# Block 0's plain columns of x: one load, or two loads on two queues, with its first products in halves

## The chip, the cores and the metric

The kernel runs on one core of a Trainium2 chip. The metric is the device time of one execution in microseconds (us). Runs of the two kernels are compared by their medians; one further execution of each is taken by the hardware profiler, and its times are those of the views quoted below. The core's engines are TensorE (PE in the views, with its weight loads as PEld), VectorE (DVE), ScalarE (ACT), GpSimd (POOL) and SyncE (SP). SP and ACT issue the kernel's loads and stores, each on a queue of its own, q1 and q10 in the views.

## The reference, cut to what matters

The output is a gated sum of two branches over x of 2048 positions and 512 features, in bfloat16:

```python
def _A_ref(x, wqkv, wo):          # sliding attention, 8 keys, 2 apart
    qkv = (x @ wqkv).reshape(B, S, 3, H, Dh)
    ...
    return o @ wo
def _B_ref(x, w1, b1, w2, b2):    # layer norm, then an MLP over the positions
    ...
g = _sigmoid((x * gate_w).sum(-1, keepdims=True))
return g * _A_ref(x, wqkv, wo) + (1 - g) * _B_ref(x, w1, b1, w2, b2)
```

The change lies in the first step of all, the product x @ wqkv for the first 512 positions.

## The kernel before, in words

The whole of x, the weights and what comes between are held on the core. Work is written as a list of operations with their engine, an estimated duration, and the names of what each reads and writes. A planner (`_Sched`) sorts them: it goes through the list by estimated start times and gives each engine one fixed order of operations, and each operation the semaphore waits that its inputs ask for. Loads have an estimated landing time in this plan (`lands`), which decides the order alone; on the chip an operation waits for the real landing. Some orders are written out by hand with `chain`.

The products contract over the 512 features in four groups of 128, called d = 0 to 3 here. As `x @ wqkv` needs x with features on the partitions, x is loaded transposed into `XT`, in blocks of 512 positions. For block 0 this is split: the features 128 to 511 (d = 1 to 3) come by a transposing load (`ld_xt0`, L473), while the features 0 to 127 (d = 0) come as they are, the plain columns, into `XP` (`d_xp`, L479). PE transposes these itself: four products with an identity (`f_tr`, L545), the first two into PSUM bank 5 (`tr0`), the other two into bank 6 (`tr1`). ACT copies the first half, positions 0 to 255, to `XT` (`ev_tra`, L555), DVE the second half, positions 256 to 511 (`ev_trb`, L557).

Ahead of the transposes, PE runs products with constants whose results nobody reads (`f_warm`, L537): six of 512 positions (`warm1`), one of 256 (`warm2`), and after the transposes one of 512 (`warm3`).

Then come the products of block 0 (`f_proj`, L619). Four banks take Q first: d = 0 for the four output tiles, then d = 1, d = 2, d = 3; then four banks take K, d = 0 and 1, then d = 2 and 3. All are of 512 positions. The first four need both copies and Wq's first quarter (rows 0 to 127 of Q's weights, `ld_w(0, 0, 1, "act")`); the second four need the transposed columns and Wq's second quarter.

The queues at the start: SP issues `d_xp`, then the transposed columns, then Wq's third and fourth quarters, K's weights in two halves, and the first tiles of x in plain form for the layer norm. ACT issues Wq's first and second quarters and then loads the table for its first activation.

Behind block 0, PE works through the other products of Q, K and V; two bursts of logit sums (L698) for which DVE multiplies Q and K (L690); the two products of the MLP (L812, L862); and the output product (L878), which DVE combines with the MLP's result (L899). The place of the bursts among PE's other products is set by the planner's estimates.

Of the kernel before, what the change touches and what calls it, by code (L numbers as in the profile page):

```python
# [333 lines left out]
def bass_gated_mix__sliding_local_dilated__mixer_token_mlp__prompt_kernel(nc, A_x, A_wqkv, A_wo, B_x, B_w1, B_b1, B_w2, B_b2, gate_w, out, dbg=None):  # L334
    with contextlib.ExitStack() as es:
# [3 lines left out]
        sch = _Sched()  # L339

        x2d = A_x[0]
        xv = x2d.rearrange("(t p) d -> p t d", p=128)
# [72 lines left out]
        A = sch.add  # L415
# [12 lines left out]
        def mk_dma(dst, src):  # L428
            return lambda e: e.dma_start(dst, src)

        init_dmas = []
# [32 lines left out]
        XT0 = ["xt0_%d" % d for d in range(4)] + ["xt0_0b"]  # L464
        ALLXT = XT0 + ["xt_%d" % t for t in range(4, NST)]

        def xt_of(sb, d0=0, d1=4):
            return XT0[d0:d1] + (XT0[4:] if d0 == 0 else []) if sb == 0 else ["xt_%d" % t for t in range(4 * sb, 4 * sb + 4)]

        def ld_xt0():  # L470
            ds = sch.dsem("xt0")
# [4 lines left out]
            return op  # L476

        XP = view("OUTS", BF16, [(128, 4), (1, 128)])
        d_xp = sch.dma("sp", mk_dma(XP, xv[:, 0:4, 0:128]), 512 * 128 * 2, sch.dsem("xp"), writes=["outs0"], issue=0.4, name="d_xp")  # L479
        d_xp.lands = 3.9  # L480
        init_dmas.append(d_xp)

        first_loads = [ld_w(0, 0, 1, "act"), ld_xt0(), ld_w(0, 1, 1, "act"), ld_w(0, 2, 1), ld_w(0, 3, 1), ld_w(1, 0, 2), ld_w(1, 2, 2),
                       ld_x(0, 2)]
        ld_xt(1)
        first_loads.append(init_dmas[-1])
        for op_, t_ in zip(first_loads, (3.5, 5.7, 5.0, 6.3, 6.7, 7.6, 8.6, 9.4, 11.0)):
            op_.lands = t_
            op_.deps.clear()
        first_loads[2].order.add(first_loads[0])  # L490
        init_dmas[:] = [first_loads[1]] + first_loads[5:]
        ld_x(2, 2)
# [8 lines left out]
        def ld_w1(j):  # L501
# [4 lines left out]
            if j < 4:  # L506
# [8 lines left out]
                       writes=["wo"], deps=throttle(), after=prev_dma(), name="d_wo")  # L515
# [4 lines left out]
        for i_, (v_, n_) in enumerate(((B_b1, NFT), (B_b2, NST))):  # L520
            vr = v_.rearrange("(t q j) -> q t j", q=4, j=32)
            for q_ in range(4):
                sch.dma("sp", mk_dma(psub(BR, 32 * q_, n_, 32 * i_, [(1, 32)]), vr[q_]), n_ * 64, ds_b, reads=["br"],
                        writes=["br_%d_%d" % (i_, q_)], deps=throttle(), after=prev_dma(), name="d_b_%d_%d" % (i_, q_), issue=0.45)
        d_w1.append(ld_w1(3))
        A("dve", lambda e: e.transpose(out=BT, in_=BR), 0.2, reads=["br_%d_%d" % (i_, q_) for i_ in range(2) for q_ in range(4)],
          writes=["btc"], name="t_b")
# [5 lines left out]
        def f_warm(n, w_=D):  # L533
            def fn(e):
                ins = None
                for _ in range(n):
                    ins = e.matmul(ps[:, 7, 0:w_], lhsT=CONE[:, 0:128], rhs=CONE[:, 0:w_], start=True, stop=True)  # L537
                return ins
            return fn

        def f_tr(h):
            def fn(e):
                ins = None
                for t in range(2):
                    ins = e.matmul(ps[:, 5 + h, 128 * t:128 * t + 128], lhsT=XP[:, 2 * h + t, :], rhs=IDENT, start=True, stop=True)  # L545
                return ins
            return fn

        A("pe", f_warm(6), 2.56, writes=["lg7_0", "lg7_1"], name="warm1", prio=-100)
        w2_ = A("pe", f_warm(1, 256), 0.2, writes=["lg7_0", "lg7_1"], name="warm2", prio=-100)  # L550
        ta_ = A("pe", f_tr(0), 0.215, reads=["outs0", "ident"], writes=["lg5_0", "lg5_1"], after=[w2_], name="tr0", prio=-100)
        tr_ = A("pe", f_tr(1), 0.215, reads=["outs0", "ident"], writes=["lg6_0", "lg6_1"], after=[ta_], name="tr1", prio=-100)
        A("pe", f_warm(1), 0.43, writes=["lg7_0", "lg7_1"], after=[tr_], name="warm3", prio=-100)
        w3_ = tr_
        A("act", lambda e: e.activation(out=XT[:, 0, 0:256], in_=ps[:, 5, 0:256], func=AF.Copy), 0.35, reads=["lg5_0", "lg5_1"],  # L555
          writes=["xt0_0"], name="ev_tra", prio=0)
        A("dve", lambda e: e.tensor_copy(out=XT[:, 0, 256:512], in_=ps[:, 6, 0:256]), 0.35, reads=["lg6_0", "lg6_1"],  # L557
          writes=["xt0_0b"], name="ev_trb", prio=0)
# [12 lines left out]
        for hf in range(2):  # L571
            t0 = 8 * hf
            for t in range(t0, t0 + 8):
                A("dve", (lambda t_: (lambda e: e.bn_stats(out=ST6[:, t_, :], in_=X[:, t_, :])))(t), 0.59,  # L574
                  reads=["x%d" % t], writes=["st6_%d" % t], name="ln1_%d" % t, prio=0)
# [13 lines left out]
              reads=["zc%d" % hf], writes=["sd%d" % hf], name="ln_sqrt%d" % hf, prio=0)  # L589
            A("dve", (lambda t0_: (lambda e: e.reciprocal(out=cols(RSTD, t0_, 8), in_=cols(SD, t0_, 8))))(t0), 0.25,  # L590
              reads=["sd%d" % hf], writes=["rstd%d" % hf], name="ln_rstd%d" % hf, prio=0)
# [40 lines left out]
        tnames = ["q", "k", "v"]  # L632
        first = [(tn, dl) for tn in range(2) for dl in range(4)]
        fbn = [["acc%d" % b] for b in range(4)] + [["lg%d_0" % b, "lg%d_1" % b] for b in range(4, 8)]
        for (b0, d0, d1, s0, s1) in ((0, 0, 1, 0, 512), (0, 1, 2, 0, 512), (0, 2, 3, 0, 512), (0, 3, 4, 0, 512), (4, 0, 2, 0, 512), (4, 2, 4, 0, 512)):
            for b in range(b0, b0 + 4):
                tn, dl = first[b]
                last_main[0] = A("pe", f_proj(tn, dl, 0, b, d0, d1, s0, s1), 0.216 * (d1 - d0) * (s1 - s0) / 512,
                                 reads=xt_of(0, d0, d1) + ["wqkv%d_%d" % (tn, dt) for dt in range(d0, d1)],
                                 writes=fbn[b], after=[last_main[0]], name="pf_%s%d_%d_%d" % (tnames[tn], dl, d0, s0))  # L640
                last_main[0].order.add(w3_)
        for b, (tn, dl) in enumerate(first):
            A("act", f_evq(tn, dl, 0, b), 0.52, reads=fbn[b] + (["k5pad"] if tn == 1 else []),
              writes=["%s5_%d_0" % (tnames[tn], dl)], name="ev_%s%d_0" % (tnames[tn], dl), prio=0)
# [7 lines left out]
        for (tn, dl, sb) in seq_proj:  # L652
# [3 lines left out]
                             reads=xr + ["wqkv%d_%d" % (tn, dt) for dt in range(4)],  # L656
# [15 lines left out]
        for t in range(NST):  # L672
# [5 lines left out]
          writes=["th"], name="g_tanh", prio=0)  # L678
# [150 lines left out]
        for ft in range(NFT):  # L829
# [6 lines left out]
              name="gel_%d" % ft, prio=0)  # L836
# [216 lines left out]
```

## Time and profile before

| | us |
|---|---|
| median of 3 runs (lowest to highest) | 167.93 (167.91 to 168.16) |
| profiled execution: its time | 168.55 |
| profiled execution: its span | 167.3 |
| PE busy in the span | 163.9 (98%) |
| DVE busy in the span | 151.3 (90%) |
| ACT busy in the span | 75.0 (45%) |

A span runs from the first to the last instruction that the profiler recorded. Matmuls are pipelined: a row's duration covers filling and draining, so the spacing of their starts, not their durations, says how fast PE works. An entry such as "idle 0.41 <-PE" names what ended the wait of an engine. In a timeline the rows are start, duration, engine, line, operation, output<-input, form and count; neighbours of one kind are merged into one row. The view of the chain that ended last is read backwards from the end of the span, and printed in order of time.

### The profile page before, as it was taken

What the parts mean: (1) busy time and instruction counts of PE and PEld (TensorE: products, weight loads), DVE (VectorE), ACT (ScalarE), POOL (GpSimd) and SP (SyncE); (2) the same over time, 40 slices, a digit from 0 to 9 for tenths busy, and PEclk for the clock granted to TensorE, in tenths of its full rate; (3) what the DMA queues carried; (4) which work ended last, traced back from release to release, by engine and by line L of the source; (5) the groups of instructions that cost most, each with busy time, mean ns of one, the idle gap of its engine ahead of it and who ended that gap; (6) DMA issues with size and microseconds to landing.
All of it is one profiled execution on the core that took longest, in us unless ns stands there. A gap on an engine that the chain in (4) does not pass through costs nothing.

```text
span 167.3 us, 2152 instructions
## 1 busy us (share of the span) xinstructions
PE 163.9 (98%) x860; PEld 77.6 (46%) x860; DVE 151.3 (90%) x154; ACT 75.0 (45%) x116; POOL 0.7 (0%) x8
## 2 busy tenths in 40 slices
PE   7999999999999999999999999999999999999994
PEld 2455555554454444444444444444444444444463
DVE  0145999999999999999999999999999999999896
ACT  3077688889899818793113121131231321310100
POOL 1000000000000000000000000000000000000000
DMA  5999999968003837996579936462672580000454
GB/s 130 315 272 262 303 322 291 307 196 246 0 0 97 311 115 187 303 290 153 133 183 343 335 129 143 112 187 68 184 218 83 138 223 0 0 0 0 157 190 159
DMA packets 47625, 29.64 MB, mean 177 GB/s; under 512 B 9856, under 2 KB 46464, under 8 KB 47616
## 3 DMA queue, kind: packets, MB, share of 16 engines
q1 hardware_dynamic: 45504, 24.85, 54.0%
q10 hardware_dynamic: 2112, 4.66, 10.0%
q8 instruction: 7, 0.11, 0.3%
q14 instruction: 2, 0.02, 0.0%
HBM read 21.24 MB, written 2.10 MB: 140 GB/s over the span
## 4 chain that ended last, share of the span: by engine, by line
PE 94%; DVE 3%; DMA 2%; issue 0%
PE ps L812 29%; PE ps L862 29%; PE ps L619 25%; PE ps L878 6%; PE ps L698 4%; DVE arena L899 2%; DMA arena<-in_A_x_dram 2%; PE ps L545 0%; DVE arena L557 0%
## 5 line engine op out<-in xcount | busy, mean ns | idle before, releaser
L812 PE MATMUL ps<-arena 128*128 128x512 bf16 x224 | 48.7, 379 | 0.0
L862 PE MATMUL ps<-arena 128*128 128x512 bf16 x224 | 48.7, 379 | 0.0
L619 PE MATMUL ps<-arena 128*128 128x512 bf16 x192 | 42.3, 382 | 0.1
L690 DVE TENSOR_TENSOR arena<-arena 128x4096 bf16<-128x4096 bf16 (+1 forms) x12 | 35.5, 2996 | 2.3 <-ACT arena L630 1.8
L797 DVE TENSOR_TENSOR arena<-arena 128x8192 bf16<-128x8192 bf16 x8 | 35.0, 4419 | 0.0
L812 PEld LDWEIGHTS ps<-arena 128*128 128x128 bf16 x224 | 21.8, 98 | 26.7 <-ACT arena L728 0.4
L862 PEld LDWEIGHTS ps<-arena 128*128 128x128 bf16 x224 | 21.9, 98 | 26.5
L619 PEld LDWEIGHTS ps<-arena 128*128 128x128 bf16 x192 | 21.6, 114 | 20.8 <-DVE arena L557 0.7
L930 ACT ACTIVATE arena<-ps,arena 128x512 bf16<-128x512 f32 x16 | 12.4, 778 | 39.4 <-PE ps L862 39.4
L800 DVE TENSOR_TENSOR arena<-arena 128x4096 bf16<-128x4096 bf16 (+1 forms) x16 | 27.0, 1752 | 0.0
L630 ACT ACTIVATE arena<-ps 128x512 bf16<-128x512 f32 x32 | 18.5, 596 | 4.5 <-PE ps L619 4.5
L833 ACT ACTIVATE arena<-ps,arena 128x512 bf16<-128x512 f32 x14 | 9.6, 687 | 22.2 <-PE ps L812 17.4
L574 DVE BATCH_NORM_STATS2 arena<-arena 128x6 f32<-128x512 bf16 x16 | 10.0, 680 | 5.6 <-DMA arena<-in_A_x_dram 5.6
L878 PE MATMUL ps<-arena 128*128 128x512 bf16 (+1 forms) x80 | 14.2, 337 | 0.0
L899 DVE SCALAR_TENSOR_TENSOR arena<-ps,arena 128x512 bf16<-128x512 f32 (+1 forms) x20 | 11.5, 638 | 0.9 <-PE ps L878 0.7
L598 ACT ACTIVATE arena<-arena 128x512 bf16<-128x512 bf16 x16 | 12.2, 806 | 0.0
L627 ACT ACTIVATE arena<-ps 128x512 bf16<-128x512 f32 x16 | 9.0, 596 | 5.5 <-PE ps L619 5.4
L878 PEld LDWEIGHTS ps<-arena 128*128 128x128 bf16 x80 | 7.8, 98 | 6.3
L674 DVE SCALAR_TENSOR_TENSOR arena<-arena 128x512 bf16<-128x512 bf16 x16 | 10.1, 685 | 0.0
L744 DVE TENSOR_TENSOR arena<-arena 128x512 bf16<-128x512 bf16 (+4 forms) x11 | 7.3, 667 | 0.6 <-ACT arena L763 0.2
L698 PE MATMUL ps<-arena 128*32 128x512 bf16 x128 | 7.3, 380 | 0.0
L728 ACT ACTIVATE arena<-ps 128x512 bf16<-128x512 f32 x8 | 4.7, 592 | 4.6 <-PE ps L698 4.6
(42 smaller groups left out, 40.5 us busy)
## 6 DMA issues: line engine op xcount, KB each, us to landing
arena<-in_B_w_dram SPq DMA_DIRECT2D x7, 1024.0 KB, 8.3
arena<-in_B_w_dram SPq DMA_DIRECT2D x8, 896.0 KB, 5.1
arena<-arena ACTq DMA_DIRECT2D x32, 128.0 KB, 3.0
arena<-in_A_x_dram SPq DMA_DIRECT2D x4, 512.0 KB, 5.1
out_dram<-arena SPq DMA_DIRECT2D x14, 128.0 KB, 1.7
arena<-in_A_x_dram SPq DMA_DIRECT2D x1, 1536.0 KB, 7.9
arena<-in_A_wqkv_dram SPq DMA_DIRECT2D x2, 256.0 KB, 3.6
arena<-in_A_x_dram SPq DMA_DIRECT2D x2, 256.0 KB, 3.5
```

What stands on the lines that cost most here:

```text
L598: A("act", (lambda t_: (lambda e: e.activation(out=X[:, t_, :], in_=X[:, t_, :], func=AF.Identity, scale=col(RSTD, t_), bias=col(NMR, t_)) ...
L619: ins = e.matmul(ps[:, bank, s0:s1], lhsT=lhsT, rhs=XT[:, dt, sb * 512 + s0:sb * 512 + s1], start=(dt == 0 and s0 == 0), stop=(dt == 3))
L630: return lambda e: e.activation(out=dst, in_=ps[:, bank, :], func=AF.Copy)
L690: return lambda e: e.tensor_tensor(out=PBL[buf][:, :, 512 * c0:512 * (c0 + nc_)], in0=in0, in1=in1, op=ALU.mult)
L698: ins = e.matmul(ps[32 * c:32 * c + 32, 4 + wl, :], lhsT=RP, rhs=PBL[buf][:, wl, c * 512:(c + 1) * 512], start=(dl == 0), stop=(dl == 3), ...
L797: A("dve", (lambda o_, i0, i1: (lambda e: e.tensor_tensor(out=o_, in0=i0, in1=i1, op=ALU.mult)))(pv, in0, in1), 4.4, reads=v_res + ["atx_% ...
L800: A("dve", (lambda pv_, n__: (lambda e: e.tensor_tensor(out=pv_[:, 0:n__], in0=pv_[:, 0:n__], in1=pv_[:, n__:2 * n__], op=ALU.add)))(pv, n ...
L812: ins = e.matmul(ps[:, bank, :], lhsT=W1W[:, slot, st, 128 * e_:128 * e_ + 128], rhs=X[:, st, :], start=(st == 0), stop=(st == NST - 1))
L862: ins = e.matmul(ps[:, bank, :], lhsT=W2S[slot][:, ft, 128 * e_:128 * e_ + 128], rhs=UT[:, ft, :], start=(ft == 0), stop=(ft == NFT - 1))
L878: ins = e.matmul(ps[:, bank, 0:c1 - c0], lhsT=OT[:, t, 128 * i:128 * i + 128], rhs=WO[:, t, c0:c1], start=(t == 0), stop=(t == 3))
L899: A("dve", (lambda i_, b_, c0_, c1_: (lambda e: e.scalar_tensor_tensor(out=T1[:, i_, c0_:c1_], in0=ps[:, b_, 0:c1_ - c0_], scalar=col(G, i ...
L930: A("act", (lambda i_, bank_: (lambda e: e.activation(out=T1[:, i_, :], in_=ps[:, bank_, :], func=AF.Identity, scale=col(OMG, i_), bias=co ...
```

## The change

`d_xp` becomes a list of two loads of 256 pieces each: the tiles 0 and 1 (positions 0 to 255) on SP, the tiles 2 and 3 on ACT, both first on their queues. `tr0` waits for the first alone, `tr1` for the second alone. Wq's first quarter is issued on ACT behind the second of them, and Wq's second quarter behind that. `warm2` is gone and `warm3` has 256 positions in place of 512; the first product of block 0 comes behind `warm3`, where it came behind `tr1` in the order that the planner was given. The four products with d = 0 for Q are cut in two: four over positions 0 to 255, which read `ev_tra`'s half alone, then four over 256 to 511, which read `ev_trb`'s. The planned landing times are given anew.

```diff
-        def xt_of(sb, d0=0, d1=4):
-            return XT0[d0:d1] + (XT0[4:] if d0 == 0 else []) if sb == 0 else ["xt_%d" % t for t in range(4 * sb, 4 * sb + 4)]
+        def xt_of(sb, d0=0, d1=4, s0=0, s1=512):
+            if sb:
+                return ["xt_%d" % t for t in range(4 * sb, 4 * sb + 4)]
+            return (XT0[d0:d1] if d0 or s0 == 0 else []) + (XT0[4:] if d0 == 0 and s1 == 512 else [])
...
-        d_xp = sch.dma("sp", mk_dma(XP, xv[:, 0:4, 0:128]), 512 * 128 * 2, sch.dsem("xp"), writes=["outs0"], issue=0.4, name="d_xp")
-        d_xp.lands = 3.9
-        init_dmas.append(d_xp)
+        d_xp = [sch.dma(q, mk_dma(XP[:, 2 * h:2 * h + 2, :], xv[:, 2 * h:2 * h + 2, 0:128]), 256 * 128 * 2, sch.dsem("xp%d" % h),
+                        writes=["outs0%s" % "ab"[h]], issue=0.4, name="d_xp%d" % h) for h, q in enumerate(("sp", "act"))]
+        for op_ in d_xp:
+            op_.lands = 3.5
+        init_dmas.append(d_xp[0])
...
-        for op_, t_ in zip(first_loads, (3.5, 5.7, 5.0, 6.3, 6.7, 7.6, 8.6, 9.4, 11.0)):
+        for op_, t_ in zip(first_loads, (4.2, 5.7, 4.7, 6.1, 6.5, 7.5, 8.4, 9.1, 11.0)):
             op_.lands = t_
             op_.deps.clear()
+        first_loads[0].order.add(d_xp[1])
         first_loads[2].order.add(first_loads[0])
...
-        A("pe", f_warm(6), 2.56, writes=["lg7_0", "lg7_1"], name="warm1", prio=-100)
-        w2_ = A("pe", f_warm(1, 256), 0.2, writes=["lg7_0", "lg7_1"], name="warm2", prio=-100)
-        ta_ = A("pe", f_tr(0), 0.215, reads=["outs0", "ident"], writes=["lg5_0", "lg5_1"], after=[w2_], name="tr0", prio=-100)
-        tr_ = A("pe", f_tr(1), 0.215, reads=["outs0", "ident"], writes=["lg6_0", "lg6_1"], after=[ta_], name="tr1", prio=-100)
-        A("pe", f_warm(1), 0.43, writes=["lg7_0", "lg7_1"], after=[tr_], name="warm3", prio=-100)
-        w3_ = tr_
+        w1_ = A("pe", f_warm(6), 2.56, writes=["lg7_0", "lg7_1"], name="warm1", prio=-100)
+        ta_ = A("pe", f_tr(0), 0.215, reads=["outs0a", "outs0", "ident"], writes=["lg5_0", "lg5_1"], after=[w1_], name="tr0", prio=-100)
+        tr_ = A("pe", f_tr(1), 0.215, reads=["outs0b", "outs0", "ident"], writes=["lg6_0", "lg6_1"], after=[ta_], name="tr1", prio=-100)
+        w3_ = A("pe", f_warm(1, 256), 0.2, writes=["lg7_0", "lg7_1"], after=[tr_], name="warm3", prio=-100)
...
-        for (b0, d0, d1, s0, s1) in ((0, 0, 1, 0, 512), (0, 1, 2, 0, 512), (0, 2, 3, 0, 512), (0, 3, 4, 0, 512), (4, 0, 2, 0, 512), (4, 2, 4, 0, 512)):
+        for (b0, d0, d1, s0, s1) in ((0, 0, 1, 0, 256), (0, 0, 1, 256, 512), (0, 1, 2, 0, 512), (0, 2, 3, 0, 512), (0, 3, 4, 0, 512), (4, 0, 2, 0, 512), (4, 2, 4, 0, 512)):
...
-                                 reads=xt_of(0, d0, d1) + ["wqkv%d_%d" % (tn, dt) for dt in range(d0, d1)],
+                                 reads=xt_of(0, d0, d1, s0, s1) + ["wqkv%d_%d" % (tn, dt) for dt in range(d0, d1)],
```

## The prediction

> **What bounds the kernel now.** I read the table of runs first, then the chain of work that ended last, then the opening of the timeline engine by engine, then the DMA queues in short windows. The profiled execution took 168.55 us, its span 167.3 us, so 1.25 us lie around the span; the median of the runs is 167.93 us. I work out a shift of the span and take it off the median. The chain in order of time (start, us, what):
>
> ```profile
> 0.80 3.10 DMA arena<-in_A_x_dram
> 3.91 0.14 issue
> 4.04 0.60 PE ps L545 x4
> 4.66 0.44 DVE arena L557
> 5.15 33.44 PE ps L619 x152
> ```
>
> The reader is to see one load (the plain columns of x, issued at 0.80, landed at 3.91), four transposes, one copy, and from 5.15 on TensorE (PE) alone. PE has no idle time worth a tenth of a microsecond behind 5.15, so what starts its products earlier moves the end, if nothing new stops it on the way. Its first products, each row the one that was running in a window of a few hundredths of a microsecond:
>
> ```profile
> 5.15 0.61 PE L619 MATMUL ps<-arena 128*128 128x512 bf16 x1
> 5.56 0.63 PE L619 MATMUL ps<-arena 128*128 128x512 bf16 x1
> 5.98 0.45 PE L619 MATMUL ps<-arena 128*128 128x512 bf16 x1
> 6.26 0.38 PE L619 MATMUL ps<-arena 128*128 128x512 bf16 x1
> 6.48 0.38 PE L619 MATMUL ps<-arena 128*128 128x512 bf16 x1
> ```
>
> The starts are 0.41, 0.42, 0.28 and 0.22 us apart: the array begins at about half rate (0.427 us for 512 positions, also the spacing of the warm-up products from 0.84) and ends at 0.216. The granted clock says 1.00 throughout, so only the spacing tells it. The 0.28 is a mixture: x at the slow rate and the rest at the fast one, x + (1 - x/0.427) 0.216 = 0.28, gives x = 0.13, so the rate rose at 5.98 + 0.13 = 6.11. A microsecond gained before 6.11 is, if the rise stays where it is, worth only 1 - 0.216/0.427 = 0.49 us at the end.
>
> **The change part by part.**
>
> *The load in two halves.* Today the one load has 512 pieces of 256 bytes. The queues in two windows, 1.9 to 2.93 and 1.9 to 3.4 (q1 is SP's, q10 ACT's; packets, bytes, share of the 16 engines):
>
> ```profile
> q10 hardware_dynamic: 95, 0.10, 34.2%
> q1 hardware_dynamic: 260, 0.07, 27.6%
> ...
> q10 hardware_dynamic: 200, 0.19, 41.4%
> q1 hardware_dynamic: 523, 0.13, 38.1%
> ```
>
> SP's queue had moved 260 packets by 2.93 and its 512 and most of the closing ones by 3.4; the load landed 0.51 after that. Half the pieces alone would land at 2.93 + 0.51 = 3.44. In the first window the engines are at 62%, so they do not pace it. Bounds for SP's half: at best it is there when PE ends the six warm-up products (3.35, the start of the seventh), at worst at 3.91 as now. ACT's half: its queue moved nothing before 2.24 (a window from 1.9 to 2.24 lists q1 alone), 0.3 later than SP's; 256 pieces at SP's 250 per us end at 3.27 and land at 3.78, at the 560 per us of 2.93 to 3.4 at 3.21. I take 3.5; the half only has to be there by 3.91 for its copy (below). The Trainium skill, "DMA: Bandwidth & Descriptors", "Issuing engines are not separate DMA queues", says that issuing on several engines saves only the time of initiating, as the same 16 engines do the work; by it the sum would be that of my first rival, 167.80. This case's trace has the engines at 62% here, so the rule's ground, engines that are full, is not met in this window.
>
> *From landing to the first product.* Now the ACT row of the evacuation:
>
> ```profile
> 0.80 1.02 ACTq L429 DMA_DIRECT2D arena<-in_A_wqkv_dram  x2
> 1.84 1.28 ACT L555 ACT_TABLE_LOAD   x1 [1.84 <-issue]
> 4.45 0.38 ACT L555 ACTIVATE arena<-ps 128x256 bf16<-128x256 f32 x1 [1.32 <-PE ps L545]
> 4.66 0.42 DVE L557 CAST arena<-ps 128x256 bf16<-128x256 f32 x1 [3.17 <-PE ps L545]
> ```
>
> ACT starts 0.54 after the landing and takes 0.38; the wait for DVE's copy ends 0.06 before the first product. The pieces need ACT's half only: 3.44 + 0.54 + 0.38 + 0.06 = 4.42, against 5.15. Bounds: 3.35 for PE free gives 4.28, and 4.5 if the wait on ACT is 0.08 slower than that on DVE (0.14 stands between landing and first transpose). ACT has one more DMA to issue, 0.43 to 0.55 by its two now, so the table load ends at 3.12 + 0.43..0.55 = 3.55 to 3.67, hidden before 3.98, when ACT is wanted. Without that cover (a landing before 3.1) it would be the next bound.
>
> *Wq's first quarter moves behind.* It is issued when the second quarter is now (1.26), which landed 3.0 later: 4.26. Bounds: 2.9 gives 4.16, a slip by one issue of 0.46 gives 4.72. With 0.14 to the product: 4.40, so the two inputs come together; I take 4.43. The second quarter moves by one issue, to about 4.8, wanted at 6.1: free.
>
> *The first four products in eight pieces.* Four more products and weight loads, the same positions: 8 x 0.213 at half rate, weight loads of 0.15 beneath (at full rate 0.108 against 0.11: at most 0.02 us in all). The last four wait for DVE's copy, which ends 1.18 behind its landing (5.09 - 3.91): 3.5 + 1.18 = 4.68, wanted at 4.43 + 0.85 = 5.28; even a landing at 3.91 hides. The shorter warm-up (one of 256 positions gone from before the transposes, one of 512 cut to 256 behind them) lies in waits: 0.21 + 0.21 us of PE off the path; its worth for the clock is a rival.
>
> *The transposed columns.* SP issues them second as now (1.29, landed 4.4 later at 5.7); behind a shorter first issue, not later. But 256 packets now stand ahead of Wq on ACT's queue, so as much of Wq falls into its time: 1519 q1 packets took 117% of 1.5 us x 16 engines in the window from 3.5 to 5.0, 0.0185 us each, so 256 x 0.0185 / 16 = 0.30 at most: 5.7 to 6.0. They are wanted after the eight pieces: 7.9 pieces at 0.213 from 4.43 reach 6.11, the rest runs at the fast rate: 6.12. Hidden, by 0.1 in the worst case. The later SP loads slip by at most 0.3 too: the second half of K's weights, issued before 5.07 and 3.6 to landing by the table of DMA issues, is there by 8.7 and wanted after twenty more products, near 10.8.
>
> *Sum.* (5.15 - 4.43) x 0.49 = 0.35 us. Does it reach the end? The rows that could stop it:
>
> ```profile
> 32.88 4.49 DVE L690 TENSOR_TENSOR arena<-arena 128x4096 bf16<-128x4096 bf16 x2
> 38.52 3.64 PE L698 MATMUL ps<-arena 128*32 128x512 bf16 x64
> 42.20 4.43 DVE L690 TENSOR_TENSOR arena<-arena 128x8192 bf16<-128x8192 bf16 x1 [0.41 <-PE ps L698]
> ...
> 157.36 0.75 DVE L899 SCALAR_TENSOR_TENSOR arena<-ps,arena 128x512 bf16<-128x512 f32 x1 [0.72 <-PE ps L878]
> ```
>
> PE's burst of logits sums at 38.52 needs DVE's products, over at 37.37: 1.15 of slack. DVE idles 0.41 for the burst's end at 42.20, so it moves along by 0.35; at the tail it waits 0.72 for PE, so it does not hold it. The plan's order behind the block: in both kernels the planner lets the second group start on the transposed columns, booked at 5.7, so its order of PE should stay. 167.93 - 0.35 = **167.58 us**.
>
> **The rivals.** *Halves that land no earlier*, or Wq late: with 3.91 the first product starts at 3.91 + 0.98 = 4.89, with Wq at 4.72 at 4.86: 0.27 x 0.49 = 0.13, so 167.80. For it: shared engines, ACT's late start; against: the 62%. *The transposed columns late*, at 6.4 instead of 5.7: the second group starts at 6.45 as now, 167.95; it needs more than twice the 0.30 worked out. *The clock rises later* (the other side): place, PE before 6.11; point, a pause before the first piece longer than the 0.30 us between the last warm-up (4.42 + 0.43 = 4.85) and 5.15, which starts the count anew. Half rate lasted 5.27 us (0.84 to 6.11); counted from 4.43 it ends at 9.70: 3.59 x 0.49 = 1.76 lost, 0.35 gained, 169.34. For it: less warm-up; against: the new pause is about 4.15 to 4.43. The Trainium skill, "TensorE: Matmul & The Clock Gate", Part 1, has a free-running window of 3.4 us that must be busy; the rise here, 5.27 us behind the first product, agrees with it, and by it one more window would end near 9.5 (an estimate). *The clock rises earlier*, if it counts work done: 0.29 us earlier, 167.43. *A burst moves by one group of products* in the plan: 0.86 later, DVE's slack of 0.72 gives way, about 167.8 or a little above 168.
>
> **How the numbers follow.** Forecast 0.62, own range 167.45 to 167.70; halves or Wq late 0.14; columns late 0.07; clock later 0.08; clock earlier 0.05; burst 0.04. What a measurement can tell here is about 0.2%, 0.34 us; the forecast lies on its edge. Faster by over 0.2% (under 167.59): 0.45 of the forecast and the early clock, 0.50. Within: 0.17 of the forecast, 0.14, 0.04 of the columns, 0.02: 0.37. Slower: 0.08 + 0.03 + 0.02 = 0.13. The range 167.3 to 168.05 takes in all but the late clock and the extremes.
>
> **What would show it.** Right: the chain's DMA piece ends at 3.4 to 3.5, ACT's L555 starts near 4.0, the first L619 row of 128x256 at 4.4 to 4.5, spacing 0.21 for eight, the first 512-wide one at 6.1 to 6.2. Wrong: a DMA piece ending at 3.9; a wait of PE on Wq or on the transposed columns after the pieces; a spacing of 0.43 beyond 6.5; a new idle row of DVE or PE behind 38.

## The result, and the profile after

| | before | after |
|---|---|---|
| median of 6 runs (lowest to highest), us | 168.16 (167.91 to 168.29) | 169.66 (168.99 to 171.21) |
| ratio of the runs, 95% interval | | 1.0100 (1.0070 to 1.0131) |
| profiled execution: time, span, us | 168.55, 167.3 | 171.21, 169.9 |

The change makes the kernel slower by 1.0%, and its runs spread over 2.2 us in place of 0.4. The ratios, here and below, leave out runs more than 1.5% above the fastest of their kernel, which the medians still count; a ratio need not equal the quotient of the two medians. The opening of the chain that ended last, after (start, us, what):

```profile
0.80 0.45 SPq L429
1.25 0.06 issue
1.31 6.26 DMA arena<-in_A_x_dram
7.57 0.05 issue
7.61 8.17 PE ps L622 x30
```

The plain columns are gone from it. In their place stands the other load of x, the transposed columns: issued at 1.31, landed at 7.57, where it had landed at 5.7. PE's own rows, and ACT's, in the timeline:

```profile
2.34 1.28 ACT L558 ACT_TABLE_LOAD   x1 [2.34 <-issue]
3.35 0.63 PE L550 MATMUL ps<-arena 128*128 128x128 bf16 x4
3.81 0.39 ACT L558 ACTIVATE arena<-ps 128x256 bf16<-128x256 f32 x1 [0.18 <-PE ps L550]
4.34 1.06 PE L622 MATMUL ps<-arena 128*128 128x256 bf16 x8 [0.23 <-DMA arena<-in_A_wqkv_dram]
7.61 0.61 PE L622 MATMUL ps<-arena 128*128 128x512 bf16 x1 [2.21 <-DMA arena<-in_A_x_dram]
```

All that the change was made for is there: the transposes start when the warm-up ends, ACT's copy at 3.81, the eight pieces at 4.34. Then PE idles 2.21 us for the transposed columns, and its second group starts at 7.61 in place of 6.48. The windows of PE's clock (us, busy time and count of PE, PEld, DVE, ACT and POOL, then PEclk, the DMA share and GB/s):

```profile
0.49:3.90 3.41, 3.06 (x11) 1.29 (x11) 0.29 (x1) 1.38 (x2) 0.56 (x5) 1.00 0.57 106
3.90:7.31 3.41, 1.27 (x10) 0.80 (x8) 0.42 (x1) 0.29 (x1) 0.00 (x0) 1.00 1.19 169
7.31:10.73 3.42, 3.12 (x8) 1.17 (x9) 0.07 (x1) 0.00 (x0) 0.00 (x0) 0.50 1.14 332
```

Here the record shows the clock: half from 7.31 to 10.73, behind the window in which PE was busy for 1.27 us of 3.41. So the second group also starts slow. (The 1.00 of the first window can't be taken at its word: the warm-up products in it start 0.42 us apart, twice the 0.216 of the full rate. The rate rose at its end, and the eight pieces start 0.11 apart.) The account of this execution: 7.61 - 6.48 = 1.13 us from the late start, and (10.73 - 7.61) x 0.49 = 1.53 from the half rate, 2.66 together; the spans differ by 2.6. The three shortest runs (168.99, 169.06, 169.39) are 0.8 to 1.2 above the median of before, about what the late start alone costs; the two longest (170.94, 171.21) are 2.8 to 3.1 above it, a little more than what both cost; 169.93 lies between. That both of the longest had the half rate fits their recorded mean clock, 0.99 in these two and 1.00 in the other four, but only 171.21 has a profile.

Why are the columns late? The queues from 3.5 to 5.0 us (packets, MB, share of 16 engines), before and then after:

```profile
q1 hardware_dynamic: 1519, 0.39, 117.2%
q10 hardware_dynamic: 51, 0.04, 7.5%
```

```profile
q1 hardware_dynamic: 646, 0.17, 64.8%
q10 hardware_dynamic: 116, 0.11, 37.8%
```

With 65 more packets on ACT's queue (q10), SP's (q1) moved 873 fewer. At the durations of before that does not balance: 65 x 0.075 x 24 / 51 = 2.3 us of the 16 engines' 24, against 873 x 1.172 x 24 / 1519 = 16 us. So the packets did not just trade places.

The experiments start from theory A: Wq's second quarter, issued 0.6 us later than before, moves on ACT's queue beside the transposing load, and slows that load and itself far beyond its own size. Its rivals: B, the two halves of x on two queues slow the load; D, the two queues only share the engines' time, as the prediction had it; P, the loss comes from the products in pieces.

### The profile page after: what moved, and what is told of

It reads as the page before. It is cut to its first block, busy times and chain, and to the rows that moved or that the text cites. A ratio compares the mean times of both kernels' runs of the same rounds, so it can differ in the third digit from the quotient of the medians.

```text
span 169.9 us, 2145 instructions
## 1 busy us (share of the span) xinstructions
PE 163.6 (96%) x849; PEld 78.2 (46%) x863; DVE 151.3 (89%) x154; ACT 75.1 (44%) x116; POOL 0.7 (0%) x8
## 4 chain that ended last, share of the span: by engine, by line
PE 92%; DMA 4%; DVE 2%; issue 1%; SPq 0%
PE ps L865 28%; PE ps L815 28%; PE ps L622 25%; PE ps L881 6%; PE ps L701 4%; DMA arena<-in_A_x_dram 4%; DVE arena L902 2%; SPq L429 0%
## 5 line engine op out<-in xcount | busy, mean ns | idle before, releaser
L865 PE MATMUL ps<-arena 128*128 128x512 bf16 x220 | 48.5, 379 | 0.2
L815 PE MATMUL ps<-arena 128*128 128x512 bf16 x219 | 48.2, 379 | 0.4 <-issue 0.2
L622 PE MATMUL ps<-arena 128*128 128x512 bf16 (+1 forms) x192 | 43.1, 384 | 2.8 <-DMA arena<-in_A_x_dram 2.2
L881 PE MATMUL ps<-arena 128*128 128x512 bf16 (+1 forms) x79 | 14.1, 336 | 0.1
L601 ACT ACTIVATE arena<-arena 128x512 bf16<-128x512 bf16 x16 | 12.2, 804 | 0.0
```

The costliest lines, as they stand in the source:

```text
L601: A("act", (lambda t_: (lambda e: e.activation(out=X[:, t_, :], in_=X[:, t_, :], func=AF.Identity, scale=col(RSTD, t_), bias=col(NMR, t_)) ...
L622: ins = e.matmul(ps[:, bank, s0:s1], lhsT=lhsT, rhs=XT[:, dt, sb * 512 + s0:sb * 512 + s1], start=(dt == 0 and s0 == 0), stop=(dt == 3))
L815: ins = e.matmul(ps[:, bank, :], lhsT=W1W[:, slot, st, 128 * e_:128 * e_ + 128], rhs=X[:, st, :], start=(st == 0), stop=(st == NST - 1))
L865: ins = e.matmul(ps[:, bank, :], lhsT=W2S[slot][:, ft, 128 * e_:128 * e_ + 128], rhs=UT[:, ft, :], start=(ft == 0), stop=(ft == NFT - 1))
L881: ins = e.matmul(ps[:, bank, 0:c1 - c0], lhsT=OT[:, t, 128 * i:128 * i + 128], rhs=WO[:, t, c0:c1], start=(t == 0), stop=(t == 3))
```

## The experiments

Eighteen kernels ran, in five jobs; in each job the kernel before ran on the same chip (medians 168.30, 168.23, 168.36, 168.50 and 168.19). "Columns" is when the transposed columns landed, "2nd group" when PE began it, in the profiled execution; it is left blank where nothing below rests on it. Each profile is of a single execution; the loads of the changed kernel, unchanged in e2 and e7, put the columns at 7.57, 7.3 and 7.8, those of the kernel before, unchanged in e1, at 5.7 and 5.8. "..." in a diff stands for lines left out. The diffs of e2, e3, e4, e6, e7 and e8 are against the kernel after, those of e1, e5 and e9 against the kernel before; the others name what they start from.

| run | columns | 2nd group | median, us | ratio to before (95%) |
|---|---|---|---|---|
| e1_pieces_only | 5.8 | 6.5 | 168.39 | 1.0001 (0.9988 to 1.0014) |
| e2_loads_only | 7.3 | 7.4 | 169.20 | 1.0065 (1.0033 to 1.0097) |
| e3_wq1_on_sp | 5.8 | 6.5 | 168.83 | 1.0045 (1.0022 to 1.0068) |
| e4_halves_on_sp | 6.0 | 6.7 | 168.52 | 1.0029 (1.0002 to 1.0056) |
| e5_late_wq1 | 5.8 | 6.0 | 168.50 | 1.0004 (0.9980 to 1.0028) |
| e6_wq1_ahead | 5.8 | 6.1 | 168.19 | 1.0005 (0.9976 to 1.0034) |
| e7_warm_gap | 7.8 | 7.8 | 169.66 | 1.0067 (1.0043 to 1.0092) |
| e8_half_dose | 6.4 | 6.8 | 169.16 | 1.0076 (1.0043 to 1.0110) |
| e9_wq1_waits | 7.0 | 7.0 | 169.80 | 1.0139 (1.0084 to 1.0194) |
| e10_xt_first | 5.1 | 5.6 | 168.11 | 0.9995 (0.9980 to 1.0011) |
| e11_ahead_warm | 5.7 | 5.9 | 168.43 | 1.0008 (0.9996 to 1.0020) |
| e12_plain_only | 4.6 | | 168.65 | 1.0029 (0.9988 to 1.0070) |
| e13_quarters_swapped | 5.2 | | 170.40 | 1.0097 (1.0055 to 1.0139) |
| e14_first_waits | 7.6 | | 173.34 (2 runs) | 1.0311 (1.0251 to 1.0370) |
| e15_waits_less | 5.7 | | 168.52 | 1.0010 (0.9992 to 1.0027) |
| e16_xt_first_w1 | 5.1 | | 168.26 | 1.0025 (0.9992 to 1.0058) |
| e17_xt_first_w2 | 4.8 | | 169.53 | 1.0059 (1.0004 to 1.0113) |
| e18_xt_first_w3 | 4.5 | | 169.00, 172.34 | none |

**The two halves of the change, each alone.** e1 is the kernel before with the products in pieces, e2 the kernel after with them whole:

```diff
 e1 against before:  (0, 0, 1, 0, 512)  ->  (0, 0, 1, 0, 256), (0, 0, 1, 256, 512)
 e2 against after:   the reverse
```

> The kernel before with the first four products cut into pieces of 256 positions, and nothing else. Theory A (Wq's two quarters, moved behind 256 small pieces on ACT's queue, now move beside the transposing load and slow it and themselves): loads as before, so the transposed columns land near 5.7 us, the first piece starts near 4.9, and the time is 0 to 0.2 us under that of before. Rival P (the pieces, with four more weight loads, cost the time): 169 us or more.

> The changed kernel with the first four products whole again (512 positions); the loads stay as changed. Theory A: the transposed columns and Wq's second quarter land after 7 us as in the changed kernel, PE idles for about 2 us before its second group, and the time is 169 to 171 us. Rival P (the pieces cost the time): back to 168.2 or less.

e1 stays at 1.0001: the pieces alone cost nothing and bring nothing that can be told. e2 has the late columns (7.3) and most of the loss from the loads alone. Rival P falls.

**Wq's second quarter off ACT's queue.**

```diff
-first_loads = [ld_w(0, 0, 1, "act"), ld_xt0(), ld_w(0, 1, 1, "act"), ...
+first_loads = [ld_w(0, 0, 1, "act"), ld_xt0(), ld_w(0, 1, 1), ...
```

> The changed kernel with Wq's second quarter issued on SP right behind the transposing load instead of on ACT; only Wq's first quarter is left to move beside that load. Theory A: the transposed columns land at 5.5 to 6.3, Wq's second quarter some 0.4 later, PE's idle time before the second group falls from 2.2 to 0.5 to 1.2 us, the time is 167.8 to 168.6 us. Rival B (the transposing load is late because it starts earlier, right behind the halves of the plain columns, whatever ACT's queue carries): the transposed columns still land near 7.5 and the time stays at 169 to 171 us.

The columns land at 5.8, 4.5 us behind their issue and with the two halves of x still on two queues. Rival B falls. The time lies a little above what was expected, and the quarter now comes last, at 6.36:

```profile
3.09 3.27 DMA arena<-in_A_wqkv_dram
6.36 0.14 issue
6.50 32.27 PE ps L622 x148
```

This second group starts where that of before did in its profile. But in an execution whose clock rises early, before's could start at 6.01 (worked out in the next section; e5 below, with the loads of before and an early rise, starts it at 6.01) and e3's still waits until 6.50; that may be the 0.5 us by which its median is above.

**Both halves on SP, Wq first on ACT as before.**

```diff
-... for h, q in enumerate(("sp", "act"))]
+... for h, q in enumerate(("sp", "sp"))]
 ...
-        first_loads[0].order.add(d_xp[1])
```

> The changed kernel with both halves of the plain columns issued on SP, one behind the other, and Wq's two quarters first on ACT as before. Theory A: Wq is done before the transposing load is in full swing, as before; the transposing load is issued one issue (0.45 us) later and lands near 6.1; the first piece starts near 4.5; no idle time of PE over 0.3 us before the second group; the time is 167.5 to 168.0 us. Rival B (halves ahead of the transposing load delay it): lands after 7 us, 169 us or more.

The columns land at 6.0, as theory A has it, and rival B falls again. The first piece missed: it came at 5.02, since the second half landed only at 4.57, later than the whole load did before (3.91), and PE's order puts its transposes ahead of the pieces. The time missed with it: 168.52, above the 167.5 to 168.0 expected.

**The suspected cause alone, in the kernel before.** The first try put an activation between ACT's two issues:

```diff
+        pre_ = A("act", lambda e: e.activation(out=col(SD, 0), in_=<ones>, func=AF.Copy), 1.5, ...)
+        pre_.order.add(first_loads[0])
+        first_loads[2].order.add(pre_)
```

> The kernel before, with one small activation on ACT between the issues of Wq's first and second quarter (it brings the table load forward), so that the second quarter is issued at about 2.8 instead of 1.3 us and moves while the transposing load is under way. Nothing else is changed. Theory A (plain packets on ACT's queue beside the transposing load slow both far beyond their own size): the transposed columns land at 6.5 to 7.6 instead of 5.7, Wq's second quarter lands with them and not at 5.8, the time is 168.7 to 170.5 us. Rival D (the 0.30 us of the prediction, engines shared by the packets' own time, is right and the two halves of x cause the rest): the columns land at 5.7 to 6.1, Wq's quarter at 5.8, the time at most 168.6 us.

It tells nothing of the theories, because the second issue was not later. ACT issued it at 1.33, while its table load was under way:

```profile
1.27 1.28 ACT L490 ACT_TABLE_LOAD   x1 [1.27 <-PEq L1040]
1.33 0.39 ACTq L429 DMA_DIRECT2D arena<-in_A_wqkv_dram  x1
```

The second try makes the issue wait for PE's second warm-up product:

```diff
-        A("pe", f_warm(6), 2.56, ..., name="warm1", prio=-100)
+        w0_ = A("pe", f_warm(2), 0.85, ..., name="warm0", prio=-100)
+        first_loads[2].deps.add(w0_)
+        w1_ = A("pe", f_warm(4), 1.7, ..., after=[w0_], name="warm1", prio=-100)
 ...
```

> The kernel before, but Wq's second quarter is issued on ACT only when PE has ended its second warm-up product (the six are listed as two and four), at about 1.95 us, as late as the changed kernel issues it (1.86). Loads of x, order and products are those of before. Theory A: this alone brings the delay: the transposed columns land at 6.5 to 7.6, the quarter with them, PE idles 0.4 to 1.5 us between its first and second group, 168.6 to 170.5 us. Rival D (the halves of x on two queues are needed for it): columns at 5.7 to 6.1, 168.0 to 168.6 us.

Now the quarter was issued at 1.88, and nothing else of the kernel before was changed, apart from listing the six warm-up products as two and four. The columns land at 6.99, PE idles 0.72 us, and the ratio is 1.014:

```profile
1.31 5.68 DMA arena<-in_A_x_dram
6.99 0.05 issue
7.04 32.13 PE ps L621 x148
```

Its queues from 3.5 to 5.0 show the same picture as after, with 932 packets on SP's where before had 1519, beside 64 on ACT's:

```profile
q1 hardware_dynamic: 932, 0.24, 104.8%
q10 hardware_dynamic: 64, 0.06, 22.2%
```

So the quarter's 0.6 us of delay brings the loss without any of the rest of the change, and e3 shows that without it the rest of the change does not delay the columns. Rival D, and with it the prediction's 0.30 us, falls. How large the harm is, and when, is another question, taken up below.

**Ahead of the transposing load, on its own queue.**

```diff
+        wq1_ = ld_w(0, 1, 1)
-        first_loads = [ld_w(0, 0, 1, "act"), ld_xt0(), ld_w(0, 1, 1, "act"), ...
+        first_loads = [ld_w(0, 0, 1, "act"), ld_xt0(), wq1_, ...
         ...
-        first_loads[2].order.add(first_loads[0])
```

> The changed kernel with Wq's second quarter issued on SP ahead of the transposing load, behind the first half of the plain columns; ACT carries the second half and Wq's first quarter. Theory A: the second quarter lands near 3.5 to 4.3 and the columns at 5.8 to 6.3, as one issue (0.45) stands ahead of them; PE's second group starts at 6.1 to 6.4; 167.8 to 168.4 us. Rival: a plain load ahead of the transposing one on the same queue slows it just as one beside it: columns after 7, 169 us or more.

The same 128 packets, ahead of the load on SP instead of beside it on ACT, do no harm: columns at 5.8, although they are issued 0.5 later (1.81). PE has its second group 0.39 us earlier than before, and yet the time is that of before (168.19 against 168.23); the section on the prediction says why.

**Half the packets.** Rows 0 to 63 of the quarter on ACT, the rest on SP behind the transposing load:

```diff
-first_loads = [ld_w(0, 0, 1, "act"), ld_xt0(), ld_w(0, 1, 1, "act"), ...
+first_loads = [ld_w(0, 0, 1, "act"), ld_xt0(), ld_wh(0, "act"), ld_wh(1, "sp"), ...
 ...
```

> The changed kernel with Wq's second quarter in two loads: rows 0 to 63 on ACT as changed (64 packets of 1024 bytes in place of 128), rows 64 to 127 on SP right behind the transposing load. If the delay goes by the number of packets beside the transposing load, the columns land half way between 5.8 (none of them) and 7.3 to 7.6 (all), at 6.5 to 6.8. If any transfer beside it switches the load to a slow way of moving, they land near 7.3. If the order at which Wq's first quarter ends counts alone, at 5.8.

Columns at 6.4, between the ends and nearest to the count of packets. It is weak evidence: from 3.9 to 4.8 only one packet moved on ACT's queue, and 80 (the load's 64 and its closing ones) from 4.8 to 5.5, so the dose fell on the end of the transposing load alone.

**The clock's share.** Six warm-up products in PE's gap:

```diff
+            if (d0, s0) == (0, 256):
+                last_main[0] = A("pe", f_warm(6), 1.3, writes=["lg7_0", "lg7_1"], after=[last_main[0]], name="warm4")
```

> The changed kernel with six more warm-up products of 512 positions on PE between the eight pieces and the second group, where PE idles for 2.2 us. Theory A with the clock as its second part (the idle time is 1.1 us of the loss; what is more, in some executions, is a stretch at half rate that the idle time brings on): no stretch at half rate behind the second group's start, all runs near 169.1 to 169.4, none over 170. Rival (the spread comes from the loads): the spread stays 169 to 171.

Half right. No run is over 170 (169.17 to 169.93, five runs, where after had 168.99 to 171.21), and the profiled execution has no stretch at half rate behind the second group. But the median is that of the changed kernel, because the columns landed no earlier (7.8 in its profile); the gain is in the spread alone, and five runs are few for that.

**Versions meant to beat both.** e10 puts the transposing load first on SP with Wq's second quarter behind it, the plain columns in one load first on ACT with Wq's first quarter behind, and the products in pieces; e11 is e6 with `warm3` of 512 positions.

```diff
 e10 against before, with e1's pieces
-d_xp = sch.dma("sp", mk_dma(XP, xv[:, 0:4, 0:128]), ...)
+d_xp = sch.dma("act", mk_dma(XP, xv[:, 0:4, 0:128]), ...)
-init_dmas.append(d_xp)
-first_loads = [ld_w(0, 0, 1, "act"), ld_xt0(), ld_w(0, 1, 1, "act"), ...
+first_loads = [ld_w(0, 0, 1, "act"), ld_xt0(), ld_w(0, 1, 1), ...
-first_loads[2].order.add(first_loads[0])
+first_loads[0].order.add(d_xp)
 ...
 e11 against e6
-w3_ = A("pe", f_warm(1, 256), 0.2, ..., name="warm3", prio=-100)
+w3_ = A("pe", f_warm(1), 0.43, ..., name="warm3", prio=-100)
```

> A version meant to beat both: the transposing load first on SP, Wq's second quarter right behind it; the plain columns in one load first on ACT, Wq's first quarter behind; the first four products in pieces. By theory A nothing but the first quarter's 128 packets stands beside the transposing load, which starts 0.5 us earlier: columns at 5.2 to 5.6, first piece at 4.9 to 5.1, second group at 5.8 to 6.2; 167.7 to 168.3 us. Rival: with the plain columns' 512 small packets beside it the load is slowed as well: columns after 6.5, 168.8 us or more.

> The kernel with Wq's second quarter on SP ahead of the transposing load (two runs above), with the last warm-up product of 512 positions instead of 256, so that the pause before the first piece is shorter. If the transposed columns' landing near 5.8 is what bounds PE's second group in the executions where the clock is up by then, this gains nothing in the median over that kernel: ratio to before 0.998 to 1.001. If the earlier first piece is what counts (half of 0.7 us), ratio 0.997 to 0.998.

In e10 the columns land at 5.1, the second group starts at 5.6, both a little earlier than expected, and the span is 166.7. But the interval of its ratio (0.9980 to 1.0011) holds no change: it beats the changed kernel, not with certainty the one before. e11 is at 1.0008, as its first case has it, so an earlier first piece is not what counts. But its profile does not show the columns as the only bound: the second group started at 5.87, right behind them (5.73), and then PE idled 0.79 us, until 7.68, for Wq's third quarter, which landed at 7.63 there and at 6.17 in e6, issued at 3.40 and 3.36. Why it was so late in that execution is open.

**What decides the size of the harm.** In e10 a quarter of Wq (the first) also moved beside the transposing load on ACT's queue, and the columns were early all the same. Four kernels ask why. e12 is e10 with both quarters on SP behind the transposing load, so that it has no quarter beside it; e13 is e10 with the quarters exchanged; e14 is e9 with the quarters exchanged, so that the first is the one held back; e15 is e9 with a shorter delay.

```diff
 e12 against e10
-first_loads = [ld_w(0, 0, 1, "act"), ld_xt0(), ld_w(0, 1, 1), ...
+xt0_ = ld_xt0()
+first_loads = [ld_w(0, 0, 1), xt0_, ld_w(0, 1, 1), ...
 ...
-first_loads[0].order.add(d_xp)
 e13 against e10
+wqa_ = ld_w(0, 1, 1, "act")
+xt0_ = ld_xt0()
+first_loads = [ld_w(0, 0, 1), xt0_, wqa_, ...
 ...
-first_loads[0].order.add(d_xp)
+first_loads[2].order.add(d_xp)
 e14 against e9
-first_loads[2].order.add(first_loads[0])
+first_loads[0].order.add(first_loads[2])
-first_loads[2].deps.add(w0_)
+first_loads[0].deps.add(w0_)
 e15 against e9
-w0_ = A("pe", f_warm(2), ...
+w0_ = A("pe", f_warm(1), ...
-w1_ = A("pe", f_warm(4), ...
+w1_ = A("pe", f_warm(5), ...
```

> The version with the transposing load first on SP, with both of Wq's quarters behind it on SP, so that ACT carries the plain columns alone. It gives the landing of a transposing load with no packet of 1024 bytes beside it. Theory H1 (every such packet beside the load costs it, however the quarter is called): columns 0.4 to 0.7 us earlier than with one quarter on ACT (5.1), at 4.4 to 4.7. Theory H3 (a quarter beside the load did nothing there, and the harm needs something else that this version lacks): 5.0 to 5.2. The time is not the point: Wq's first quarter comes late.

> The version with the transposing load first on SP, with Wq's second quarter in the place of the first on ACT, and the first behind the transposing load. H1: columns as in that version, 4.8 to 5.4. Theory H2 (it is the second quarter's rows, whose reads or writes collide with those of x, that slow the load): columns at 5.9 or later.

> The kernel before with Wq's second quarter first on ACT and the first quarter held back till PE's second warm-up product, at 1.9 us: the run in which the second quarter waited (columns at 7.0), with the quarters swapped. H1: columns at 6.4 to 7.4. H2: columns at most 6.1, as the second quarter is gone by then.

> The kernel before with Wq's second quarter held back till PE's first warm-up product, at about 1.45 us in place of 1.3 (before) and 1.9 (columns at 7.0). H1, by the share of its packets that are left when the transposing load starts: columns at 5.8 to 6.4. A step rather than a slope (harm whenever the quarter is issued behind the transposing load's issue at 1.3): 6.7 to 7.3.

e12 gives the load with no quarter beside it: 4.64, so in e10 the quarter costs 0.47 us, not far above its own time (128 packets of 0.042 us over 16 engines, 0.34). It is not the particular quarter: exchanged, the columns land at 5.2 in e13 and at 7.6 in e14, somewhat later than expected (both lose time besides because Wq's first quarter is late). And a small delay does nothing: with the issue at 1.46 in e15 the columns land at 5.7, as before, which neither of its two expectations had, and with it at 1.88 in e9 at 7.0. Whether the harm between the two comes at an edge or grows was not tested. The queues from 3.3 to 3.9 show two ways in which the two kinds of packet pass; first before and e10, then after:

```profile
q1 hardware_dynamic: 340, 0.09, 63.4%
q10 hardware_dynamic: 119, 0.11, 52.6%
```

```profile
q10 hardware_dynamic: 128, 0.12, 63.6%
q1 hardware_dynamic: 258, 0.07, 48.5%
```

```profile
q1 hardware_dynamic: 190, 0.05, 63.2%
q10 hardware_dynamic: 24, 0.02, 43.4%
```

Before and in e10 most of a quarter goes through on ACT's queue in this stretch, as a burst, and SP's queue goes on behind it. After, 24 packets of ACT's queue go, the last of Wq's first quarter among them, spread between the load's, and the load too moves fewer. The engines are as busy (106% after, 116% before), so each packet takes longer: on q10 0.434 x 9.6 / 24 = 0.17 us after against 0.526 x 9.6 / 119 = 0.042 before, on q1 0.032 against 0.018 (9.6 is 0.6 us x 16 engines). This goes on for over 2 us in after, e2, e7, e9 and e14, all of which have a late landing (7.0 to 7.8).

The last three ask whether the moment of the quarter's issue, counted from that of the transposing load, brings this about: e10 with Wq's first quarter held back by one, two or three warm-up products.

```diff
 e16, e17, e18 against e10 (n = 1, 2, 3)
-A("pe", f_warm(6), 2.56, ..., name="warm1", prio=-100)
+w0_ = A("pe", f_warm(n), ..., name="warm0", prio=-100)
+first_loads[0].deps.add(w0_)
+w1_ = A("pe", f_warm(6 - n), ..., after=[w0_], name="warm1", prio=-100)
```

> The version with the transposing load first on SP (issued 0.81 to about 2.15; columns at 5.1 with Wq's first quarter issued at 1.28 on ACT, at 4.6 with no quarter beside it); here the quarter waits for PE's first warm-up product and is issued at about 1.46. Theory G (harm comes when the plain load is issued more than half a microsecond behind the start of the transposing load's issue and before its end, while the descriptors of the transposing load are being made): columns at 5.9 or later. Theory O (the overlap of packets counts, and the later the issue the smaller it is): 4.9 to 5.2.

> The same with the quarter waiting for the second warm-up product, issued at about 1.9, still before the end of the transposing load's issue. Theory G: columns at 5.9 or later. Theory O: 4.8 to 5.2.

> The same with the quarter waiting for the third warm-up product, issued at about 2.3, behind the end of the transposing load's issue but before its packets are done (2.4 to 4.1). Theory G: no more harm than the packets' own time, columns at 4.6 to 5.1. Rival (any issue behind the first half microsecond harms): 5.9 or later.

It does not. The quarter was issued at 1.46, 1.88 and 2.31, and the columns landed at 5.07, 4.77 and 4.54: the later, the less harm to the columns, as far as no harm. In e17 none of the quarter's packets is seen before 3.9, when most of the transposing load is through, and they pass in a burst too. The times of e17 and e18 rise because the first product waits for the quarter, which lands at 5.32 and 6.47. In e18, behind the columns but beside SP's plain loads, the quarter itself took 4.16 us from issue to landing, against 3.15 in e16.

What all the harmed runs have in common is a plain load ahead of the transposing one on SP, and a quarter issued on ACT some 0.55 us behind the issue of the transposing one. That this delay matters is shown by e15 (0.15 us, no harm) against e9. That the plain load ahead does is only suggested, by e16: it has none, a delay of 0.66 and no such harm, but it moves the plain columns to ACT as well. Why the packets then mix one by one instead of passing in a burst stays open. That the quarter beside the load is the cause in the changed kernel is shown; a rule for how much such a load will cost is not.

## Why the prediction was wrong

**Right: the way to the first product.** The halves landed at 3.0 and 3.2, earlier than 3.44 and ahead of the transposes' start at 3.35; the table load ended at 3.62, hidden; Wq's first quarter released PE at 4.34, where 4.40 was written for it; the first piece came at 4.34, where 4.43 was written. (One bound was mis-added: from PE free at 3.35 the rows give 3.35 + 0.41 + 0.38 + 0.06 = 4.20, not 4.28; Wq's quarter decided, so it changed nothing.) The first rival, halves that land no earlier, is out, and with it the 167.80 that the prediction took from the Trainium skill, "DMA: Bandwidth & Descriptors", "Issuing engines are not separate DMA queues". This is no evidence against the page, which does not make full engines its condition either, as the prediction read it. For the load need not be split to land early: in e10, e12, e13 and e16 to e18 it moves whole, first on ACT, and lands at 3.0 to 3.2 too. Which part the order of the loads has in that, and which the queue, no run separates. Behind the block the same waits of DVE stand in the timeline (0.41 at the burst, 0.73 at the tail), and the two terms above account for the whole loss, so it lies ahead of 10.73 and not behind it.

**Wrong: the transposed columns.** The step that failed is "so 256 x 0.0185 / 16 = 0.30 at most: 5.7 to 6.0". It added the packets' own durations, as if the engines shared by the two queues only divided their time. Measured is a landing at 7.57, 1.83 later. The row that was read for it, 3.5 to 5.0 before, is of a transposing load that had the engines nearly alone (51 packets beside 1519), so it could not price a mixture; a bound from it was called "at most" without a row that holds both kinds of traffic. e9 measures the mixture in the kernel before: 1.3 us for 128 packets (6.99 against 5.7). Where the quarter passes in a burst, the same kind of sum comes near: 128 packets cost 0.47 in e10. So the term was sized for the milder of two ways. The part on Wq's quarters gave the second one 4.8 and called it free; it landed at 7.34. "The transposed columns late" stood among the rivals, with the right place, but with 6.4 and a chance of 0.07 that both came from the same 0.30.

**Wrong in size: a microsecond is worth 0.49.** This rested on the rate rising at 6.11, as in the one profiled execution. The rise is not tied to the kernel: in after, e6 and e2 PE's warm-up products and transposes start at the same times, the last at 3.78, and it comes at 3.90, 6.76 and 10.14. Elsewhere it shows at 3.9 in e10, 5.5 in e9, 8.4 in e4 and 12.2 in e18. Where it comes before the first product, the first group takes 0.86 us and before's second group could start at 5.15 + 0.86 = 6.01; the columns, at 5.8 in e6 as before, then allow a gain of 0.2 us at most, 0.1%, however early the first piece comes. In e6's own profile the second group starts 0.39 earlier, but the rise came 0.66 later, worth 0.66 x 0.49 = 0.32, and the spans are 167.2 and 167.3. So even without the delay the 0.35 us were not there to be had. That this is what holds e6's median is worked out from these profiles, not measured run by run; e11's profile, where a later quarter stopped PE, shows that the columns need not be the only bound.

**The clock as a rival.** The half rate did come back, and cost about as much as was written for it (1.53 against 1.76), but behind PE's idle time at 5.4 to 7.6, not ahead of the first piece; e7 speaks for that cause. So in after the place and the point of that rival were wrong. In e2's profile it took the form that was written: the rate had not risen by the first product, and the products stay 0.42 us apart until 10.14. Whether the shorter warm-up or PE's waits (0.30 and 0.97 us) kept it down there is not shown, nor which form the other long runs had.

## What to carry to other kernels

A load moved to a later place on its queue is priced by what it will then move beside, not by its own landing: if that is a transposing load on another queue, put it on the same queue, ahead (e6) or behind (e3, where it then came last), where none of these runs shows the harm to the transposing load. A bound on contention needs a row in which both kinds of traffic are in flight; where none exists, the upper end is open and the chance of that rival large. When a wait is removed at the start, look which load lands next and by how much it had been hidden (here 0.2 us where the clock is up), before pricing what stood ahead of it.

## What was not expected of the hardware

Plain packets on one queue beside a transposing load on another passed in two ways, as a burst at 0.042 us a packet (before) or spread out at 0.17 (after), and a delay of the issue from 1.46 to 1.88 was enough to go from the one to the other (e15, e9).

The clock's record in after comes in stretches of 3.41 us, and the stretch with 1.27 us of PE's busy time was followed by one at half rate. The length agrees with the window in the Trainium skill, "TensorE: Matmul & The Clock Gate", Part 1; that page drops the rate after an idle window, while here a window that was busy for 37% of its length was enough. In e8 a window busy for 1.84 us (3.92 to 7.33) was not followed by half rate: its products behind are 0.22 us apart.

How full a window must be for the rise is not sharp in these runs. Where a change of rate in the record fixes where the windows of 3.41 us lie, the rate rose behind windows with PE busy for 3.06 us (after, 0.49 to 3.90) and 3.12 (e9, 2.11 to 5.52), and not behind one with 2.72 (e4, 1.57 to 4.98). In e2 two windows of 2.77 lie on either side: no rise behind the first (3.32 to 6.73), by the spacing of 0.42, and a rise behind the second (6.73 to 10.14).

ACT issued a load while its own table load was under way (1.33 against 1.27 to 2.55 in e5): the activation put ahead of the issue in ACT's order, which ran at 2.56, did not hold it back. In e9, where the issue waits for PE's product, it was held back.
